# Weight conversion in pairs with an integer add, row sums from a ones column, fixed PSUM banks and another order of the beginning, in a kernel of local attention and two MLPs

## The chip, the cores and the metric

The kernel runs on one core of a Trainium2 chip. The metric is device time in microseconds (us) of one execution; the kernel before takes 1071.78 us (median of three runs). Engines are called as the profile calls them: PE (TensorE, matmul; PEld its weight loads), DVE (VectorE), ACT (ScalarE), POOL (GpSimd) and SP (SyncE, which here issues every DMA).

## What is computed

```python
# q, k, v: (4, 8, 768, 64) float32; mem_k, mem_v: 8 memory rows per head
for c in range(768 // 32):                        # chunks of 32 queries
    l, r = max(0, 32*c - 16), min(768, 32*c + 32 + 8)
    k_full = concat([mem_k, k[:, :, l:r]]); v_full = concat([mem_v, v[:, :, l:r]])
    s = q_c @ k_full.T / 8
    a = exp(s - s.max()); a = a / (a.sum() + 1e-9)
    out_c = a @ v_full
x = out.transpose(0, 2, 1, 3).reshape(3072, 512)
h = max(x @ w1, x @ w2, x @ w3)                    # 512 -> 768
y = h @ w_mid                                      # 768 -> 512
g = y @ w_in                                       # 512 -> 2048
g = where(g >= 1, g, where(g <= -1, 0, (g + 1)**2 / 4))
out = g @ w_out                                    # 2048 -> 512
```

The weights lie in DRAM as 64-bit floats. The kernel splits each matrix, activations too, into a high and a low part and multiplies with three matmuls (high by high, high by low, low by high).

## The kernel before, in words

**Work.** The 3072 tokens are 24 units of 128 and six blocks of 512 (four units each). Attention goes by unit `u`, in steps: `tk`/`ck` (transpose k on PE, copy out on ACT), `ek`, `kw` (windows of k), `tq`/`cq`, `s` (64 small score matmuls), `mx` (row maxima and subtraction, DVE), `ex` (exp, ACT), `n` (row sums, reciprocal, multiplication), `a`/`ca` (transpose), `o` (64 small matmuls with v), `co` (copy), `x`/`cx`/`dx` (transpose into the high and low halves of the MLP's input). `lk`, `lq`, `lv` load k, q and v. The first MLP takes 18 layer-one slots per block (`slot_l1`, three matrices by six 128-wide columns, 12 matmuls of 512 columns each) and six layer-two slots (`slot_l2`, also 12 matmuls); the second MLP takes 16 and 16 slots per block. All six blocks of the first MLP come before the second.

**Weights.** A 64-bit tile is fetched as 128x512 pairs of 32-bit words (`fetch_w`, 512 KB). The 24 tiles of the first MLP are made into high and low parts at the start, by `convert_w` (clear the sign, clamp, shift, merge: L137 to L143), `hi_w` (L150), `rest_w` (a correction from the lower word: L156 to L162), `sub_w` (L168) and `add_w` (L173), spread over DVE, ACT and POOL by lists of names. The 32 tiles of the second MLP are fetched and rounded to 32 bits by `round_w` (L180 to L182) between the slots of blocks 1 to 4, 30 of them are stored to DRAM (`wd`), loaded again later by `load_w` and split by `split_w`.

**Order.** Nothing is scheduled automatically: instructions run on each engine in the order of the program. `PLAN`, a list of names written out by hand, sets that order for the beginning: attention of units 0 to 3 whole and of units 4 to 8 in part, the 24 weight tiles, the first block's 18 layer-one slots (`l0` to `l17`) and five layer-two slots (`m0` to `m4`). `d` is a group of four matmuls whose result nobody reads (L723). From there on, the loop over `order` interleaves one slot, one attention step (`att_step`) and one piece of weight rounding (`round_step`).

**PSUM.** There are three pools: four banks that gather the layer-two sums, two for layer one, two for all else; in the beginning attention rotates over all of them (`psum_turn`).

Of the kernel before, what the change touches and what calls it, by code (L numbers as in the profile page):

```python
# [847 lines left out]
```

## Time and profile before

| what | value |
|---|---|
| runs | 1071.78, 1072.73, 1070.55 us; median 1071.78 |
| span of the profiled execution (first to last instruction) | 1066.3 us |
| PE busy | 1027.0 us, 96% of the span |
| DVE busy | 538.0 us, 50% |
| ACT busy | 347.8 us, 33% |
| POOL busy | 244.3 us, 23% |

The profile has no time of its own for the execution besides the span; the median of the runs lies 5.5 us above it. How to read it: PE is a pipeline and the ends of its matmuls are modelled, so the distance from one start to the next tells its pace, and a row's own duration does not. A row of the timeline gives the start, the duration, the engine and the line, and in brackets the idle time before it and what ended that.

### The profile page before, as it was taken

How to read it: one execution, taken by the hardware profiler on the slowest of the kernel's cores; microseconds unless marked ns; L12 is line 12 of the kernel's file. 1: busy time of each engine (PE TensorE's matmuls, PEld its weight loads, DVE VectorE, ACT ScalarE, POOL GpSimd, SP SyncE). 2: the span in 40 equal slices, each digit the busy share in tenths (PEclk: the TensorE clock that was granted, in tenths of full speed). 3: DMA queues.
4: the chain of work that ended last, by engine and by line, in shares of the span. 5: the costliest groups of instructions: out<-in, count | busy, mean ns of one | idle time of the engine just before them, and what ended most of it. 6: DMA issues, size and time to landing. Idle time of an engine off the chain costs nothing.

```text
span 1066.3 us, 18296 instructions
## 1 busy us (share of the span) xinstructions
PE 1027.0 (96%) x7426; PEld 833.3 (78%) x7426; DVE 538.0 (50%) x936; ACT 347.8 (33%) x625; POOL 244.3 (23%) x194
## 2 busy tenths in 40 slices
PE   5689999999999899999999999999999999999998
PEld 4467777888888787888888888888888888888886
DVE  7888975787776777734456232232222223223222
ACT  5744444333224223233343222222222222222222
POOL 2413231010110110102123323322322322332221
PEclk9669999999999999999999999999999999999999
DMA  9764415656646554333340010001001001001001
GB/s 225 185 175 126 128 32 154 153 142 150 153 117 151 144 137 144 108 108 114 124 138 21 11 50 12 19 19 41 20 1 50 23 8 50 21 1 40 1 1 39
DMA packets 163940, 88.89 MB, mean 83 GB/s; under 512 B 126736, under 2 KB 144144, under 8 KB 163856
## 3 DMA queue, kind: packets, MB, share of 16 engines
q1 hardware_dynamic: 163856, 87.72, 30.3%
q8 instruction: 58, 0.95, 0.4%
q14 instruction: 26, 0.21, 0.1%
HBM read 67.24 MB, written 20.45 MB: 82 GB/s over the span
## 4 chain that ended last, share of the span: by engine, by line
PE 88%; DVE 6%; issue 0%; POOL 0%; ACT 0%; POOLq 0%; DVEq 0%; ACTq 0%
PE l L512 17%; PE l L514 17%; PE l L513 17%; PE o L608 8%; PE o L610 8%; PE o L609 8%; PE y L512 3%; PE y L514 3%; PE y L513 3%; PE o L433 1%; PE s L368 1%; PE ta L420 1%; PE tx L447 1%; DVE lo_a L173 1%; DVE st_a L162 0%
## 5 line engine op out<-in xcount | busy, mean ns | idle before, releaser
L596 DVE SCALAR_TENSOR_TENSOR u<-u 128x512 f32<-128x512 f32 x96 | 66.6, 694 | 351.6 <-ACT u L595 351.6
L524 POOL TENSOR_TENSOR hl_b<-u,hh_b 128x512 fp32r<-128x512 f32 x96 | 124.0, 1291 | 373.3 <-ACT hh_b L522 215.8
L512 PE MATMUL l<-xh,hi_a 128*128 128x512 f32 x432 | 176.7, 409 | 2.8 <-DVE xh L455 1.6
L514 PE MATMUL l<-xh,lo_a 128*128 128x512 f32 x432 | 170.8, 395 | 2.6 <-DVE lo_a L173 2.6
L513 PE MATMUL l<-xl,hi_a 128*128 128x512 f32 x432 | 170.4, 394 | 0.0
L512 PE MATMUL l<-yh,hi_c 128*128 128x512 f32 x384 | 150.5, 392 | 0.0
L513 PE MATMUL l<-yl,hi_c 128*128 128x512 f32 x384 | 150.4, 392 | 0.0
L514 PE MATMUL l<-yh,lo_c 128*128 128x512 f32 x384 | 150.3, 391 | 0.0
L610 PE MATMUL o<-hi_d,hl_b 128*128 128x512 f32 x384 | 150.1, 391 | 0.0
L608 PE MATMUL o<-hi_d,hh_b 128*128 128x512 f32 x384 | 150.0, 391 | 0.0
L609 PE MATMUL o<-lo_d,hh_b 128*128 128x512 f32 x384 | 150.0, 391 | 0.0
L595 ACT ACTIVATE u<-l 128x512 f32<-128x512 f32 x96 | 57.4, 597 | 229.8 <-PE l L514 191.6
L524 POOL TENSOR_TENSOR hl_a<-t,hh_a 128x512 fp32r<-128x512 f32 x34 | 47.1, 1384 | 320.8 <-ACT hh_a L522 308.8
L522 ACT CAST hh_b<-u 128x512 fp32r<-128x512 f32 x96 | 59.6, 621 | 146.8 <-DVE u L597 146.8
L514 PEld LDWEIGHTS l<-xh,lo_a 128*128 128x128 f32 x432 | 82.1, 190 | 21.4 <-DVE lo_a L173 3.5
L512 PEld LDWEIGHTS l<-xh,hi_a 128*128 128x128 f32 x432 | 82.2, 190 | 21.2 <-DVE t L540 2.3
L513 PEld LDWEIGHTS l<-xl,hi_a 128*128 128x128 f32 x432 | 82.3, 190 | 15.7 <-DVE xl L459 0.4
L514 PEld LDWEIGHTS l<-yh,lo_c 128*128 128x128 f32 x384 | 72.3, 188 | 15.9
L513 PEld LDWEIGHTS l<-yl,hi_c 128*128 128x128 f32 x384 | 72.1, 188 | 15.8
L608 PEld LDWEIGHTS o<-hi_d,hh_b 128*128 128x128 f32 x384 | 72.1, 188 | 15.7 <-ACT y L565 0.2
L512 PEld LDWEIGHTS l<-yh,hi_c 128*128 128x128 f32 x384 | 72.1, 188 | 15.6
L609 PEld LDWEIGHTS o<-lo_d,hh_b 128*128 128x128 f32 x384 | 72.2, 188 | 15.4
(126 smaller groups left out, 1327.6 us busy)
## 6 DMA issues: line engine op xcount, KB each, us to landing
st_a<-in_moe_w_dram SPq DMA_DIRECT2D x18, 512.0 KB
vw<-in_v_dram SPq DMA_DIRECT2D x160, 56.0 KB
st_c<-in_moe_w_in_dram SPq DMA_DIRECT2D x16, 512.0 KB
st_d<-in_moe_w_out_dram SPq DMA_DIRECT2D x16, 512.0 KB
yd<-y SPq DMA_DIRECT2D x24, 256.0 KB
yr<-yd SPq DMA_DIRECT2D x24, 256.0 KB
out_dram<-ob SPq DMA_DIRECT2D x24, 256.0 KB
wd<-c_c SPq DMA_DIRECT2D x16, 256.0 KB
```

The source lines that it names most:

```text
L173: e.tensor_tensor(out=weights[kind, j][1], in0=c.bitcast(F32), in1=up.bitcast(F32), op=ALU.add)
L368: nc.tensor.matmul(s[e][c * CH:(c + 1) * CH, h * NK:(h + 1) * NK], qTb[u % 2][r, h, c], kw[r, h, c, 0:NK], start=True, stop=True)
L512: nc.tensor.matmul(ps, whi, xhi, start=first, stop=False)
L513: nc.tensor.matmul(ps, whi, xlo, start=False, stop=False)
L514: nc.tensor.matmul(ps, wlo, xhi, start=False, stop=last)
L522: nc.scalar.copy(out=hi, in_=h)
L524: e.tensor_tensor(out=lo, in0=h, in1=hi.bitcast(F32), op=ALU.subtract)
L595: nc.scalar.activation(out=a, in_=ps, func=AF.Relu, bias=0.5, scale=0.5)
L596: nc.vector.scalar_tensor_tensor(out=a, in0=a, scalar=1.0, in1=a, op0=ALU.min, op1=ALU.mult)
L608: nc.tensor.matmul(acc[t], hi[:, c], whi, start=first, stop=False)
L609: nc.tensor.matmul(acc[t], hi[:, c], wlo, start=False, stop=False)
L610: nc.tensor.matmul(acc[t], lo[:, c], whi, start=False, stop=last)
```

## The change

It has five parts. (1) Weights are handled in pairs of tiles (128x1024). The high word is cleared, clamped, shifted and merged as before, but the correction from the low word is now an integer: ACT multiplies the low word by 2^-29 and writes an integer (`tail_w`), and DVE adds it to the merged word (`sum_w`). High and low parts are then a copy on ACT (`wh`) and one subtraction (`ws`), on POOL but for the first two pairs. All 16 pairs of the second MLP now pass through DRAM. (2) The values get a 65th column of ones, so `o` also yields the row sums; the steps `n` are gone, and `co`, now on DVE, divides while it copies. (3) The eight PSUM banks are given by number. (4) `PLAN` is another: attention's inputs are loaded first and weights later, and there are more `d` groups. (5) y is reloaded in two pieces of 512 KB per block, not four of 256 KB.

```diff
-LEAST, MOST = 2.0 ** -15, float.fromhex("0x1.dffffep+16")
+LEAST, MOST = 2.0 ** -15, float.fromhex("0x1.dffffcp+16")
 PLAN = """
-f1 d7 lk1 wa1 lk0 f0 tk0 wg1 lq1 tk1 wa0 lmem0 wh1 ws1 wg0 mem0 lq0 lm0 lk2 ck0 tq0 tq1 ek0 ck1 wh0
...
+d3 lk0 d3 d3 d3 lmem0 d3 lq0 d3 d3 tk0 lk1 mem0 ck0 lm0 lq1 tq0 cq0 lk2 tk1 mv2 d3 ck1 d3 ek1 lk3
...
-        turn[0] += 1
-        if turn[0] % 4 == 3 and turn[0] < 54:
-            st = at.tile([P, TB, 2], U32, tag="st4", name=f"st_{kind}_{j}")
-        else:
-            st = stage.tile([P, TB, 2], U32, tag="st", name=f"st_{kind}_{j}", bufs=3)
+        if q not in staged:
+            staged[q] = stage.tile([P, 2, TB, 2], U32, tag="st", name=f"st{q}", bufs=2)
...
+    def abs_w(q, c):
+        nc.scalar.activation(out=c.bitcast(F32), in_=staged[q][:, :, :, 1].bitcast(F32), func=AF.Abs)
+
+    def tail_w(q):
+        low = staged[q][:, :, :, 0]
+        nc.scalar.activation(out=low, in_=low, func=AF.Copy, scale=2.0 ** -29)
+
+    def bits_w(q, c):
...
         V.tensor_scalar(out=cf, in0=cf, scalar1=LEAST, scalar2=MOST, op0=ALU.max, op1=ALU.min)
         V.tensor_scalar(out=c, in0=c, scalar1=3, scalar2=0x3FFFFFFF,
                         op0=ALU.logical_shift_left, op1=ALU.bitwise_and)
-        V.scalar_tensor_tensor(out=c, in0=up, scalar=0xC0000000, in1=c,
+        V.scalar_tensor_tensor(out=c, in0=staged[q][:, :, :, 1], scalar=0xC0000000, in1=c,
                                op0=ALU.bitwise_and, op1=ALU.bitwise_or)
-    def rest_w(kind, j):
...
-    def sub_w(kind, j):
...
-    def add_w(kind, j):
...
+    def sum_w(q, c):
+        nc.vector.tensor_tensor(out=c, in0=c, in1=staged.pop(q)[:, :, :, 0], op=ALU.add)
+
+    def new_c(q):
+        tiles[q] = stage.tile([P, 2, TB], U32, tag="c", name=f"c{q}", bufs=2)
+        return tiles[q]
...
+    def ws(q):
+        hi, lo = split2.pop(q)
+        e = nc.vector if f"ws{q}" in ON_DVE else nc.gpsimd
+        e.tensor_tensor(out=lo, in0=tiles.pop(q).bitcast(F32), in1=hi.bitcast(F32), op=ALU.subtract)
...
+    spots = {"s": (0, 1), "o": (2, 3), "a": 4, "x": 5, "k": 6, "q": 7}
...
-            nc.vector.tensor_reduce(out=r, in_=p, axis=AX.X, op=ALU.add)
-        nc.vector.tensor_scalar(out=r, in0=r, scalar1=1e-9, scalar2=None, op0=ALU.add)
-        nc.vector.reciprocal(out=r, in_=r)
-        e = nc.gpsimd if f"n{u}" in NORM_ON_POOL else nc.vector
-        e.tensor_tensor(out=p, in0=p, in1=r.to_broadcast([P, 2 * HP, NK]), op=ALU.mult)
...
-        for e, o in enumerate(pp.pop(("o", u))):
-            copy("co", u)(
-                out=xs[u].rearrange("p (h e d) -> p e h d", h=HP, e=2)[:, e],
-                in_=o[:, 0:HP * D].rearrange("p (h d) -> p h d", h=HP))
+        for e in range(2):
+            nc.vector.tensor_scalar(out=r[:, e], in0=o[e][:, :, D:D + 1], scalar1=1e-9, scalar2=None, op0=ALU.add)
+        nc.vector.reciprocal(out=r, in_=r)
+        for e in range(2):
+            nc.vector.tensor_tensor(
+                out=x[:, e], in0=o[e][:, :, 0:D], in1=r[:, e].to_broadcast([P, HP, D]), op=ALU.mult)
...
-    BY_PART = "out in b", "", "out in", "a", "b", "a"
+    BY_PART = "out in in", "", "", "a", "", "b"
...
             if name == "l0":
-                del psum_turn[:]
-                psum_turn += [(ps_t, "t")]
+                spots["k"], spots["q"] = spots["a"], spots["x"]
+            if name == "m0":
+                spots["s"] = spots["o"] = (4, 5)
```

**SP, the first DMAs.** `kq` takes k and q, `vw`, `vxh` and `vxl` take v, `st...` are weights, x8 are the eight DMAs of one unit's v. Before:

```order
L122 DMA st_a1_0_104<-in_moe_w2_dram 128x4x256
L223 DMA kq_87<-in_k_dram 128x8x64 x2
L122 DMA st_a0_0_118<-in_moe_w1_dram 128x4x256
L229 DMA kq_87<-in_q_dram 128x8x64
L691 DMA memk_93<-in_mem_k_dram 128x2x64 x2
L229 DMA kq_87<-in_q_dram 128x8x64
L237 DMA mv0_158<-in_mem_v_dram 8x4x64 x2
L223 DMA kq_87<-in_k_dram 128x8x64
L122 DMA st_a2_0_177<-in_moe_w3_dram 128x4x256
L223 DMA kq_87<-in_k_dram 128x8x64 x2
```

and in the changed kernel, from the first DMA to the second weight tile:

```order
L653 DMA memk_95<-in_mem_k_dram 128x2x64 x2
L217 DMA kq_89<-in_q_dram 128x8x64
L211 DMA kq_89<-in_k_dram 128x8x64
L225 DMA mv0_157<-in_mem_v_dram 8x4x64 x2
L217 DMA kq_89<-in_q_dram 128x8x64
L211 DMA kq_89<-in_k_dram 128x8x64 x2
L217 DMA kq_89<-in_q_dram 128x8x64 x2
L211 DMA kq_89<-in_k_dram 128x8x64
L243 DMA vw_92<-in_v_dram 40x4x64 x2
L243 DMA vw_92<-in_v_dram 56x4x64 x6
L120 DMA st0_332<-in_moe_w1_dram 128x4x256
L217 DMA kq_89<-in_q_dram 128x8x64
```

The first weight tile goes from the first place to behind the v of unit 0; five more v and k, q loads follow between the next tiles.

**DVE, two tiles of weights.** Before, the first two tiles (`a1_0` is the first of w2, `a0_0` the first of w1; `st` is the fetched tile, `c` the converted one):

```order
L140 TENSOR_SCALAR c_a1_0_112<-c_a1_0_112 128x512
L141 TENSOR_SCALAR c_a1_0_112<-c_a1_0_112 128x512
L143 SCALAR_TENSOR_TENSOR c_a1_0_112<-st_a1_0_104,c_a1_0_112 128x512
L156 TENSOR_SCALAR st_a1_0_104<-c_a1_0_112 128x512
L162 SCALAR_TENSOR_TENSOR st_a1_0_104<-st_a1_0_104 128x512
L140 TENSOR_SCALAR c_a0_0_133<-c_a0_0_133 128x512
L141 TENSOR_SCALAR c_a0_0_133<-c_a0_0_133 128x512
L143 SCALAR_TENSOR_TENSOR c_a0_0_133<-st_a0_0_118,c_a0_0_133 128x512
L168 TENSOR_TENSOR c_a1_0_112<-c_a1_0_112,hi_a1_0_140 128x512
L156 TENSOR_SCALAR st_a0_0_118<-c_a0_0_133 128x512
L162 SCALAR_TENSOR_TENSOR st_a0_0_118<-st_a0_0_118 128x512
```

In the changed kernel, the first pair (`c0`), unit 2's division (`r2`, `xs2`) and the second pair (`c1`):

```order
L141 TENSOR_SCALAR c0_606<-c0_606 128x1024
L142 TENSOR_SCALAR c0_606<-c0_606 128x1024
L144 SCALAR_TENSOR_TENSOR c0_606<-st0_332,c0_606 128x1024
L407 TENSOR_SCALAR r2_666<-bank2_81 128x4
L407 TENSOR_SCALAR r2_666<-bank3_82 128x4
L408 RECIPROCAL r2_666<-r2_666 128x8
L410 TENSOR_TENSOR xs2_667<-bank2_81,r2_666 128x4x64
L410 TENSOR_TENSOR xs2_667<-bank3_82,r2_666 128x4x64
L148 ISA c0_606<-st0_332,c0_606 128x2048
L141 TENSOR_SCALAR c1_684<-c1_684 128x1024
L142 TENSOR_SCALAR c1_684<-c1_684 128x1024
L144 SCALAR_TENSOR_TENSOR c1_684<-st1_507,c1_684 128x1024
```

The eleven instructions of two tiles (L168 of the second and both L173 stand further on) become four of 1024 columns per pair; the add at L148 is listed over 2048 elements. These first conversions stood ahead of the first scores and now stand behind those of unit 3.

**The copy between `o` and `x` in the loop after the plan.** Before, on ACT, for unit 10 (`o10_0`, `o10_1` are its two banks):

```order
L424 COPY aT10_2465<-ta10_2460 128x512
L137 ACTIVATE c_d_0_2472<-st_d_0_2393 128x512
L439 COPY xs10_2525<-o10_0_2491 128x4x64
L439 COPY xs10_2525<-o10_1_2492 128x4x64
L455 CAST xh2_2058<-tx10_2547 128x4x128
```

In the changed kernel, on DVE, the same unit's division behind a pair's conversion (`c14`) and the maxima of a slot (`t_1_3`):

```order
L519 TENSOR_TENSOR t_1_3_2228<-bank7_86,t_1_3_2228 128x512
L141 TENSOR_SCALAR c14_2264<-c14_2264 128x1024
L142 TENSOR_SCALAR c14_2264<-c14_2264 128x1024
L144 SCALAR_TENSOR_TENSOR c14_2264<-st14_1970,c14_2264 128x1024
L519 TENSOR_TENSOR t_1_3_2228<-bank6_85,t_1_3_2228 128x512
L407 TENSOR_SCALAR r10_2315<-bank4_83 128x4
L407 TENSOR_SCALAR r10_2315<-bank5_84 128x4
L408 RECIPROCAL r10_2315<-r10_2315 128x8
L410 TENSOR_TENSOR xs10_2316<-bank4_83,r10_2315 128x4x64
L410 TENSOR_TENSOR xs10_2316<-bank5_84,r10_2315 128x4x64
```

The copy moves from ACT, behind one weight instruction of 512 columns, to DVE, behind three of 1024 and a slot's maximum.

## Rows read from the trace of the kernel before

**Rows 1.** The page, part 1: busy time of each engine

```profile
PE 1027.0 (96%) x7426; PEld 833.3 (78%) x7426; DVE 538.0 (50%) x936; ACT 347.8 (33%) x625; POOL 244.3 (23%) x194
```

**Rows 2.** Stretches: length, busy (x count) per engine, granted clock, DMA share, GB/s

```profile
0.00:20.00 20.00, 8.68 (x95) 6.71 (x96) 13.27 (x36) 11.71 (x20) 3.81 (x10) 1.00 0.97 224
20.00:40.00 20.00, 11.95 (x321) 9.10 (x327) 19.35 (x40) 13.57 (x27) 7.50 (x6) 0.82 0.86 214
...
45.00:67.70 22.70, 17.16 (x339) 13.31 (x323) 17.35 (x39) 14.65 (x29) 7.30 (x6) 0.58 0.73 182
67.70:73.20 5.50, 5.46 (x12) 3.76 (x12) 5.33 (x10) 1.24 (x2) 0.00 (x0) 0.50 0.51 141
74.80:151.60 76.80, 71.83 (x688) 56.68 (x686) 68.64 (x119) 35.92 (x68) 22.16 (x16) 1.00 0.39 110
...
151.60:351.00 199.40, 198.67 (x2114) 159.68 (x2112) 138.13 (x265) 68.53 (x128) 24.18 (x19) 1.00 0.57 141
...
600.00:700.00 100.00, 100.00 (x440) 82.27 (x439) 27.38 (x40) 24.99 (x42) 28.18 (x22) 1.00 0.07 22
```

**Rows 3.** Timeline of PE: first layer-one matmul, a stall, end of the plan

```profile
67.75 0.76 PE L512 MATMUL l<-xh,hi_a 128*128 128x512 f32 x1 [1.63 <-DVE xh L455]
...
146.46 0.50 PE L514 MATMUL l<-xh,lo_a 128*128 128x512 f32 x1 [1.56 <-DVE lo_a L173]
...
151.59 0.39 PE L512 MATMUL l<-xh,hi_a 128*128 128x512 f32 x1
```

**Rows 4.** Chain that ended last: PE's pace in a score step and a transpose

```profile
165.89 0.44 PE tx L447 x4
...
169.08 0.79 PE s L368 x53
```

**Rows 5.** Timeline of DVE just ahead of the first layer-one matmul

```profile
65.24 0.43 DVE L156 TENSOR_SCALAR st_a<-c_a 128x512 uint32<-128x512 uint32 x1 [2.47 <-POOL c_a L168]
66.31 0.68 DVE L459 TENSOR_TENSOR xl<-tx,xh 128x512 fp32r<-128x512 f32 x1
```

**Rows 6.** Timeline of SP: eight issues of v each for units 0 and 3

```profile
23.31 6.24 SPq L255 DMA_DIRECT2D vw<-in_v_dram  x8
...
43.13 4.71 SPq L255 DMA_DIRECT2D vw<-in_v_dram  x8
```

**Rows 7.** Groups of DVE: count | busy us, mean ns of one | idle before

```profile
L388 DVE TENSOR_TENSOR p<-s,m 128x256 f32<-128x256 f32 x48 | 17.9, 413 | 0.0
...
L143 DVE SCALAR_TENSOR_TENSOR c_a<-st_a,c_a 128x512 uint32<-128x512 uint32 x18 | 12.5, 692 | 0.6
...
L141 DVE TENSOR_SCALAR c_c<-c_c 128x512 uint32<-128x512 uint32 x16 | 6.8, 428 | 0.5
```

**Rows 8.** Groups of ACT and POOL, same columns

```profile
L538 ACT COPY t<-l 128x512 f32<-128x512 f32 x36 | 21.1, 585 | 49.3 <-PE l L514 45.3 <-POOL hl_a L524 4.0
...
L439 ACT COPY xs<-o 128x256 f32<-128x256 f32 x48 | 15.5, 376 | 27.6 <-PE o L433 27.0 <-PE tx L447 0.6
...
L137 ACT ACTIVATE c_a<-st_a 128x512 f32<-128x512 f32 x13 | 8.9, 681 | 14.5 <-DMA st_a<-in_moe_w_dram 5.8 <-POOL lo_a L173 3.9 <-POOL lo_b L173 3.0
...
L173 POOL TENSOR_TENSOR lo_a<-c_a,st_a 128x512 fp32r<-128x512 f32 x6 | 8.2, 1363 | 9.0 <-DVE c_a L168 5.9 <-issue 2.7
```

**Rows 9.** Timeline of DVE and of POOL at 81 us

```profile
81.24 1.31 DVE L140 TENSOR_SCALAR c_a<-c_a 128x512 f32<-128x512 f32 x1
...
80.97 1.30 POOL L173 TENSOR_TENSOR lo_a<-c_a,st_a 128x512 fp32r<-128x512 f32 x1
```

**Rows 10.** Timeline at 350 us: DVE, then PE; and the stretch behind the stall

```profile
348.66 0.43 DVE L140 TENSOR_SCALAR c_c<-c_c 128x512 f32<-128x512 f32 x1 [5.54 <-DMA vw<-in_v_dram]
...
355.49 0.20 DVE L412 RECIPROCAL r<-r 128x8 f32<-128x8 f32 x1
...
356.57 0.63 PE L420 MATMUL ta<-ident,p 128*128 128x128 f32 x4 [2.61 <-DVE p L414]
...
356.50:360.30 3.80, 3.73 (x12) 3.04 (x13) 3.73 (x8) 1.17 (x2) 0.00 (x0) 0.59 0.83 189
```

More of the change, by code (lines that the diff above doesn't have):

```diff
@@ L100, in attention_then_two_mlps @@
     wd = dram.tile([2 * K2, P, TB], F32, name="wd")
+    banks = [psum.tile([P, TB], F32, name=f"bank{i}") for i in range(8)]
     weights = {}
@@ L142, in convert_w @@
                         op0=ALU.logical_shift_left, op1=ALU.bitwise_and)
-        V.scalar_tensor_tensor(out=c, in0=up, scalar=0xC0000000, in1=c,
+        V.scalar_tensor_tensor(out=c, in0=staged[q][:, :, :, 1], scalar=0xC0000000, in1=c,
                                op0=ALU.bitwise_and, op1=ALU.bitwise_or)
-        half[kind, j] = low, up, c
-    def hi_w(kind, j, pool):
-        hi = pool.tile([P, TB], F32R, tag="w", name=f"hi_{kind}_{j}")
-        lo = pool.tile([P, TB], F32R, tag="w", name=f"lo_{kind}_{j}")
-        nc.scalar.copy(out=hi, in_=half[kind, j][2].bitcast(F32))
-        weights[kind, j] = (hi, lo)
@@ L195, in split_w, with load_w @@
+    def load_w(q):
+        n = 2 * (q - Q1)
+        staged[q] = stage.tile([P, 2, TB], F32, tag="st", name=f"w{q}", bufs=2)
+        nc.sync.dma_start(out=staged[q], in_=wd[n:n + 2].rearrange("t p f -> p t f"))
+    def split_w(q, pool):
+        new_w(q, pool)
+        t = staged.pop(q)
+        hi, lo = split2.pop(q)
         nc.scalar.copy(out=hi, in_=t)
         nc.vector.tensor_tensor(out=lo, in0=t, in1=hi.bitcast(F32), op=ALU.subtract)
-        weights[kind, j] = hi, lo
     kT2 = at.tile([P, 2, HP, LEFT + P + RIGHT], F32, name="kT2")
@@ L508, in att_step, with mm3, next_mm @@
             run(*s)
-    def mm3(ps, whi, wlo, xhi, xlo, first, last):
-        nc.tensor.matmul(ps, whi, xhi, start=first, stop=False)
-        nc.tensor.matmul(ps, whi, xlo, start=False, stop=False)
-        nc.tensor.matmul(ps, wlo, xhi, start=False, stop=last)
-    hs, cur, acc = {}, {}, {}
+    def mm3(out, whi, wlo, xhi, xlo, first, last):
+        nc.tensor.matmul(out, whi, xhi, start=first, stop=False)
+        nc.tensor.matmul(out, whi, xlo, start=False, stop=False)
+        nc.tensor.matmul(out, wlo, xhi, start=False, stop=last)
+    hs, cur = {}, {}
+    acc = banks[0:KD]
+    mm_turn = [0]
+    def next_mm():
+        mm_turn[0] += 1
+        return banks[6 + mm_turn[0] % 2]
     unsplit, stores = [], []
@@ L662, in attention_then_two_mlps, with round_step @@
-    BY_PART = "out in b", "", "out in", "a", "b", "a"
-    def w_tile(n):
-        return conv[n][1] or bp["w"]
-    def w_step(s):
-        n = ready[0]
-        while asked[0] < min(stashed, n + 3) and asked[0] < converted[0] - len(stash):
+    def round_step(acts):
+        if "out" in acts and kept:
+            q, c = kept.pop(0)
+            n = 2 * (q - Q1)
+            nc.sync.dma_start(out=wd[n:n + 2].rearrange("t p f -> p t f"), in_=c)
+        q = rounded[0]
+        if "a" in acts and q in staged:
+            abs_w(q, new_c(q))
+            tail_w(q)
+            bits_w(q, tiles[q])
+        if "b" in acts and q in tiles:
+            sum_w(q, tiles[q])
+            kept.append((q, tiles.pop(q).bitcast(F32)))
+            rounded[0] += 1
+        if "in" in acts:
+            for _ in range(acts.count("in")):
+                if fetched[0] < len(conv) and fetched[0] // 2 - rounded[0] < 2:
+                    fetch_w(fetched[0])
+                    fetched[0] += 1
```

367 lines of the change are left out of this document (143 added, 224 removed).

## The prediction

> **What bounds the kernel now.** I read the page's shares first: PE is busy for 96% of the span [rows 1], so a change that leaves the matmuls as they are can only win where PE waits. The stretches show where that is [rows 2]. Late in the run PE is busy all the time, with 440 matmuls in 100 us: 0.227 us each, 2.73 us for a slot of 12. From 151.6 us PE is full already (198.67 of 199.40). Before that it is not: between 45 and 67.7 us it is busy for 17.16 of 22.70 at a granted clock of 0.58, and DVE has no gap from 20 to 40 us (19.35 of 20.00). The timeline of PE gives the marks [rows 3]: the first layer-one matmul starts at 67.75, released by DVE; the plan's last one is over at 151.59, where the loop's first slot begins. Between them PE waits again for a low part of the weights (1.56 us at 146.46). In 74.8 to 151.6 us DVE is busy for 68.64 of 76.80 and PE for 71.83: two engines about as full as one another [rows 2]. Just ahead of the first layer-one matmul DVE still handles weights and then xl [rows 5].
>
> So the beginning is 151.6 us, and the rest, 914.7 us of the span of 1066.3, is PE's. At 151.59 and at the same slot of the changed kernel the same slots and attention steps are done, so time = end of the plan + rest. The median lies 5.5 us above the span, in work outside it that the change does not touch; I predict differences and add them to the median.
>
> **The floor of the plan after its first slot.** PE then has 18 layer-one and five layer-two slots, 23 x 2.73 = 62.8 us; seven score and `o` steps at 0.79, 5.5; eleven transposes at 0.44, 4.8 [rows 2, 4]. That is 73 us. Before, it took 151.6 - 67.75 = 84.
>
> **Weights in pairs.** DVE takes 0.413 us for two inputs of 256 columns and 0.692 for 512 [rows 7]: 0.28 per 256 more, so 1.25 for 1024 and 2.37 for 2048. One input takes 0.428 for 512, about 0.73 for 1024 if its fixed part is the same. Before, two tiles cost DVE 2 x (0.43 + 0.43 + 0.69 + 0.43 + 0.69) = 5.3 us, and 0.69 for each subtraction that was not on POOL. Now a pair costs 0.73 + 0.73 + 1.25 = 2.7 and the integer add. The trace of before has no such add. If it runs as the merge does, a word at a time, it takes 1.25; if it steps through the 2048 elements it is listed with, 2.37. I take 1.5, nearer to the merge, which also reads every second word of the fetched tile, and keep both ends.
>
> The Trainium skill's page "VectorE: DVE Perf Modes" ("What auto-detection actually checks") says that the engine takes two elements a cycle if every tensor is 16-bit with step one. By that rule the add would cost about 1.2 us, an estimate; where the skipped words break the rule, 2.3. The row gives no answer, so this is rival C below.
>
> ACT's part is hidden: per pair a clearing (0.68 for 512, some 1.1 for 1024), the low word and a copy (0.585 for 512, 0.21 per 256 more, 1.0 each) [rows 8], 3.1 us against DVE's 4.2. POOL subtracts ten of twelve pairs at 2 x 1.363 = 2.7 us [rows 8], 27 us in the stretch, hidden too unless it holds DVE. It can: at 81.24 a clamp took 1.31 us instead of 0.43, while a POOL subtraction ran from 80.97 to 82.27 [rows 9]. So each of the ten may cost DVE between nothing and its length less what had passed; at most one clamp a pair, 0.9 as measured, 9 us over ten. I take half, 4.
>
> The Trainium skill's page "SBUF — State Buffer" ("SBUF: two separate sides") states that VectorE and GpSimd share a port pair under an exclusive lock, held for the whole instruction. The two rows at 81 us agree. By that rule a doubled subtraction can hold DVE for up to 2.7 us, 27 over ten; the sum would be some 20 us later at worst.
>
> **The order of the beginning.** Attention's data come first now. Ahead of the first layer-one slot there are some 15 loads of k and q (0.26 MB), four of v (0.43 MB) and five tiles (0.52 MB), 8.3 MB; at the 224 GB/s of the first 20 us [rows 2] that is 37 us. SP needs 4.7 to 6.2 us to issue one v [rows 6], 19 to 25 for four, and these start only behind the first loads, at some 14 us; I let the fourth v land at 41. Behind it come `o` 0.8, the division 1.4 (two multiplications of 0.413 and three small operations at 0.2 [rows 7, 10]), transpose 0.44, a cast of 0.4 on ACT, and xl 0.68 [rows 5]: 3.7 us. In DVE's queue there stand between them an add (1.5), a unit's maxima and subtractions (four operations like the 0.413 one, 1.65) and a subtraction of a pair (1.25): 4.4. So the first slot starts at about 50 us against 67.75. Bounds: 45 if those were all done before the v lands, 58 if SP's later queue is as slow as its slowest row and the half clock of before's first slot (granted 0.50 [rows 2]) shows again.
>
> From there DVE has ten pairs: 10 x (2.7 + 1.5) = 42 us; twelve layer-one maxima at 0.69, 8.3; four xl, 2.7; two subtractions of h, 1.4; four divisions, 5.7; three units' maxima, 5.0. That is 65, and with POOL's holds 69. The first of the ten begins some 4 us after the first slot, since a unit's maxima and the pair's landing stand ahead; after the last add there remain a copy on ACT (1.0), POOL's subtraction (2.7) and the two slots that stand behind it (5.5), 9 us. 4 + 69 + 9 = 82, above PE's floor of 73, so DVE sets it: the plan ends at 132, **19.6 us earlier**. With the add at 2.37 it is 141, with 1.25 and no holds 125.
>
> **The rest.** Matmuls stay; the ones column makes 64 small ones a column longer, nothing against 0.79 us. The stall at 356.57 goes if nothing is late there: 2.61 us, and 0.41 of the 3.8 us at a granted clock of 0.59 behind it, 1.6 [rows 10]; DVE had waited 5.54 us there for a DMA, ahead of `n`, which is gone. Fetches and conversions move, so I count 4. Against it stands the division. PE has one slot, 2.73 us, between `o` and the transpose that waits for it; the division takes 1.4, so 1.3 may be lost in DVE's queue. Behind it in order before were ACT's two copies of 0.376 [rows 8]; now a pair's three operations (2.7) and a maximum (0.69) may be running when `o` ends. The overshoot is nothing at best and 2.7 + 0.7 + 1.4 - 2.7 = 2.1 us at worst; I take 0.45 for the 16 units that have a conversion: 7 us. Net **+3**. The y reload moves the same bytes at a DMA share of 0.07 [rows 2]: nothing.
>
> Sum: 1071.8 - 19.6 + 3 = **1055 us**.
>
> **Rivals.** A, the forecast, DVE-bound plan: 0.60, with 1045 to 1063 of its own (first slot 45 to 58, holds 0 to 9, rest 0 to 7).
>
> B: the fetches become the bound. There are two pair buffers, so the fetch of a pair waits for the add of the pair two before. One turn is 1.05 MB at the plan's 110 to 141 GB/s (9.5 to 7.4 us [rows 2]), some 2 to land, then 1.1, 2.7 and 1.5: 14.7 to 16.8 us for two pairs, 73 to 84 for ten. The plan ends at 50 + 13 + 73 to 84, 136 to 147; the time is 1059 to 1070. For it: the DMA share of 0.73 to 0.97 early on. Against it: less v and k is left to load by then. 0.17.
>
> C: the add costs 1.25 and nothing is held; PE's floor sets the end, 50 + 73 = 123, and with nothing lost in the rest the time is 1071.8 - 28.6 = 1043. For it: the merge's row. 0.12.
>
> D, slower: the division sits between `o` and the transpose on the wrong queue. 19.6 + 4 us are won, so it decides from 24 / 16 = 1.5 us per unit. At the whole overshoot of 2.1, and a clamp held by POOL's subtraction of h in front of it (0.9 [rows 9]), it is 3.0 x 16 = 48, and the time 1071.8 - 24 + 48 = 1096; the clock may fall behind each stall as at 356. For it: DVE is busy for 138 of 199 us there [rows 2]. Against it: that is 69%, and much of it was rounding that is now cheaper. 0.11.
>
> **Range.** 1041 to 1069 takes in A, C and most of B, and leaves D and B's end out. Faster by over 0.2% (about what a measurement of this kernel can tell from none) is A, B and C but for what is left of them near 1070: 0.86; within it 0.03; slower 0.11.
>
> **What would show it.** Right: the first layer-one matmul near 50 us, the loop's first slot near 132, DVE over 90% busy between them; the integer add near 1.5 us; clamps of over 1.6 us beside POOL's subtractions; small PE gaps before the transposes of x after the plan. Wrong: DVE waiting for DMA of weights in the plan (B), the add at either end of its bounds, or gaps of over 1.5 us before the transposes of x (D).

## The result and the profile after

The changed kernel takes 1054.98 us (median of four runs, 1053.55 to 1055.62); the kernel before, measured beside it, 1071.16 (four runs, 1067.14 to 1072.73). The ratio is 0.986, its 95% interval 0.9836 to 0.9885: 12 to 18 us less. The span went from 1066.3 to 1053.3, 13.0 less. The forecast was 1055.

The page of the kernel after, part 1, answers [rows 1]:

```profile
PE 1027.2 (98%) x7542; PEld 832.3 (79%) x7542; DVE 456.7 (43%) x733; ACT 350.1 (33%) x545; POOL 227.7 (22%) x172
```

PE did the same work in 13 us less. The marks of its timeline, to set beside [rows 3] (first layer-one slot, a wait for a low part, first slot of the loop, and the one stall after it):

```profile
53.01 0.48 PE L484 MATMUL bank<-xh,hi 128*128 128x512 f32 x1
...
108.86 0.50 PE L486 MATMUL bank<-xh,lo 128*128 128x512 f32 x1 [0.86 <-POOL lo L173]
...
139.59 0.51 PE L484 MATMUL bank<-xh,hi 128*128 128x512 f32 x1 [0.68 <-ACT xh L425]
...
331.82 0.66 PE L417 MATMUL bank<-ident,xs 128*128 128x128 f32 x4 [1.56 <-DVE xs L410]
```

The first slot starts 14.7 us earlier, the plan ends 12.0 earlier, the rest is 1.0 shorter (913.7 against 914.7). So from the first slot to the end of the plan it now takes longer, 86.6 against 83.8. That is no loss: nine of the 24 weight tiles had passed DVE's merge before the first slot in the kernel before, four now, and the other twenty stand in those 86.6 us. What fell is DVE's work in all. From the start to the end of the plan, before (first row) and after (second fence), columns as in [rows 2]:

```profile
0.00:151.59 151.59, 119.38 (x1539) 93.08 (x1539) 128.08 (x249) 80.71 (x151) 43.36 (x40) 0.88 0.60 152
```

```profile
0.00:139.59 139.59, 120.06 (x1654) 93.97 (x1654) 105.92 (x175) 80.27 (x120) 31.91 (x22) 1.00 0.69 174
```

DVE does in 105.9 us what took 128.1, 22 less, and it set the time in both kernels: of the chain that ended last, 48 of the 83.8 us from the first slot to the end of the plan lie on DVE before, 56 of the 86.6 after, and after that is most of the stretch from 60.6 to 115 us. A piece of it (start, length, what):

```profile
66.75 0.60 DVE t L519
67.34 1.13 DVE c L148
68.48 0.60 DVE hl_a L503
69.08 0.01 issue
69.09 0.70 DVE c L141
69.79 0.02 issue
69.81 0.70 DVE c L142
70.52 0.02 issue
70.54 3.30 DVE c L144
```

The last line is a merge that takes 1.22 us elsewhere. The groups of DVE between the first slot and the end of the plan show how often that happened (count | busy, mean ns of one | idle before):

```profile
L144 DVE SCALAR_TENSOR_TENSOR c<-st,c 128x1024 uint32<-128x1024 uint32 x10 | 16.3, 1628 | 0.3
L141 DVE TENSOR_SCALAR c<-c 128x1024 f32<-128x1024 f32 x10 | 14.1, 1411 | 0.8 <-ACT c L133 0.7
L148 DVE CUSTOM_DVE_ANT_0 c<-st,c 128x2048 uint16<-128x2048 uint16 x10 | 13.8, 1380 | 1.0
L142 DVE TENSOR_SCALAR c<-c 128x1024 uint32<-128x1024 uint32 x10 | 9.0, 903 | 0.3
```

Their medians over the run are 1.226, 0.695, 1.221 and 0.694 us, 38.3 us for ten pairs; they took 53.2. The 14.9 us beyond lie beside POOL's instructions. DVE's timeline, and POOL's:

```profile
60.50 2.68 DVE L141 TENSOR_SCALAR c<-c 128x1024 f32<-128x1024 f32 x1
...
70.54 3.29 DVE L144 SCALAR_TENSOR_TENSOR c<-st,c 128x1024 uint32<-128x1024 uint32 x1
...
76.72 0.42 DVE L372 TENSOR_TENSOR p<-bank,m 128x256 f32<-128x256 f32 x1
77.07 0.41 DVE L371 TENSOR_REDUCE m<-bank 128x4 f32<-128x256 f32 x1
77.52 0.42 DVE L372 TENSOR_TENSOR p<-bank,m 128x256 f32<-128x256 f32 x1
77.86 1.48 DVE L519 TENSOR_TENSOR t<-bank,t 128x512 f32<-128x512 f32 x2
```

```profile
60.23 2.40 POOL L173 TENSOR_TENSOR lo<-c,hi 128x1024 fp32r<-128x1024 f32 x1 [58.78 <-ACT hi L168]
70.07 2.68 POOL L173 TENSOR_TENSOR lo<-c,hi 128x1024 fp32r<-128x1024 f32 x1 [7.44 <-ACT hi L168]
76.35 2.40 POOL L173 TENSOR_TENSOR lo<-c,hi 128x1024 fp32r<-128x1024 f32 x1 [3.60 <-ACT hi L168]
```

Eight of the ten subtractions held one conversion each, five of them clamps, for 12.9 us together; two merges lost 1.0 us each to POOL's subtractions of h. The clamp at 60.50 and the merge at 70.54 lose 2 us each to a subtraction that had begun just before. Beside the third one, from 76.35 to 78.75, DVE reads PSUM (`bank`) and loses nothing.

The granted clock is 1.00 in all of the first 140 us, where it was 0.88.

### The profile page after: what moved, and what is told of

Its sections match the earlier page's. It is cut to its first block, busy times and chain, and to the rows that moved or that the text cites. A ratio compares the mean times of both kernels' runs of the same rounds, so it can differ in the third digit from the quotient of the medians.

```text
span 1053.3 us, 17983 instructions
## 1 busy us (share of the span) xinstructions
PE 1027.2 (98%) x7542; PEld 832.3 (79%) x7542; DVE 456.7 (43%) x733; ACT 350.1 (33%) x545; POOL 227.7 (22%) x172
## 4 chain that ended last, share of the span: by engine, by line
PE 87%; DVE 7%; DMA 3%; SPq 1%; issue 1%; ACT 1%; POOL 0%; DVEq 0%; POOLq 0%; ACTq 0%
PE bank L484 19%; PE bank L485 19%; PE bank L486 19%; PE bank L597 8%; PE bank L596 8%; PE bank L595 8%; DVE c L144 1%; PE bank L397 1%; DVE c L148 1%; PE bank L355 1%; DVE c L141 1%; SPq L243 1%; DMA kq<-in_k_dram 1%; DVE c L142 1%; PE bank L417 1%
## 5 line engine op out<-in xcount | busy, mean ns | idle before, releaser
L484 PE MATMUL bank<-xh,hi 128*128 128x512 f32 x432 | 174.9, 405 | 1.2 <-ACT xh L425 0.7
L486 PE MATMUL bank<-xh,lo 128*128 128x512 f32 x432 | 168.9, 391 | 1.8 <-POOL lo L173 1.8
L485 PE MATMUL bank<-xl,hi 128*128 128x512 f32 x432 | 169.0, 391 | 0.3 <-DVE xl L429 0.2
L484 PE MATMUL bank<-yh,hi 128*128 128x512 f32 x384 | 150.4, 392 | 0.0
L485 PE MATMUL bank<-yl,hi 128*128 128x512 f32 x384 | 150.2, 391 | 0.0
L486 PE MATMUL bank<-yh,lo 128*128 128x512 f32 x384 | 150.2, 391 | 0.0
L597 PE MATMUL bank<-hi,hl_b 128*128 128x512 f32 x384 | 150.0, 391 | 0.0
L596 PE MATMUL bank<-lo,hh_b 128*128 128x512 f32 x384 | 149.9, 390 | 0.0
L595 PE MATMUL bank<-hi,hh_b 128*128 128x512 f32 x384 | 149.8, 390 | 0.0
L485 PEld LDWEIGHTS bank<-xl,hi 128*128 128x128 f32 x432 | 81.3, 188 | 15.9 <-DVE xl L429 1.0
L485 PEld LDWEIGHTS bank<-yl,hi 128*128 128x128 f32 x384 | 72.2, 188 | 15.8
```

The costliest lines, as they stand in the source:

```text
L484: nc.tensor.matmul(out, whi, xhi, start=first, stop=False)
L485: nc.tensor.matmul(out, whi, xlo, start=False, stop=False)
L486: nc.tensor.matmul(out, wlo, xhi, start=False, stop=last)
L595: nc.tensor.matmul(acc[t], hi[:, c], whi, start=first, stop=False)
L596: nc.tensor.matmul(acc[t], hi[:, c], wlo, start=False, stop=False)
L597: nc.tensor.matmul(acc[t], lo[:, c], whi, start=False, stop=last)
```

## The experiments

For all of them, from PE's timeline and the spans (us; rest = span less end of the plan):

| kernel | median | ratio to before, 95% | first slot | plan ends | between | rest |
|---|---|---|---|---|---|---|
| before | 1071.16 | | 67.75 | 151.59 | 83.8 | 914.7 |
| after | 1054.98 | 0.9836 to 0.9885 | 53.01 | 139.59 | 86.6 | 913.7 |
| no fillers | 1055.44 | 0.9852 to 0.9885 | 53.95 | 140.53 | 86.6 | 913.0 |
| subtractions on DVE | 1051.12 | 0.9813 to 0.9845 | 52.02 | 134.45 | 82.4 | 913.5 |
| half subtractions | 1053.04 | 0.9833 to 0.9877 | 50.81 | 137.50 | 86.7 | 912.7 |
| add twice | 1068.74 | 0.9983 to 1.0003 | 52.71 | 152.53 | 99.8 | 913.2 |
| old correction | 1090.72 | 1.0190 to 1.0238 | 55.65 | 169.96 | 114.3 | 918.6 |
| row sums back | 1063.41 | 0.9928 to 0.9964 | 56.01 | 152.38 | 96.4 | 910.9 |
| longer division | 1075.68 | 1.0048 to 1.0086 | 50.89 | 138.92 | 88.0 | 933.5 |
| before, with fillers | 1072.73 | 1.0028 to 1.0063 | 69.85 | 157.76 | 87.9 | 914.1 |
| weights first again | 1061.32 | 0.9896 to 0.9943 | 55.39 | 143.61 | 88.2 | 916.2 |
| old correction on DVE | 1083.28 | 1.0125 to 1.0155 | 53.78 | 161.90 | 108.1 | 919.6 |
| three edits | 1045.59 | 0.9768 to 0.9815 | 50.29 | 131.29 | 81.0 | 911.3 |
| two beside PSUM | 1046.10 | 0.9765 to 0.9804 | 54.68 | 134.62 | 79.9 | 911.4 |

Beside the later ones the kernel before took 1068.0 to 1069.6. The column of the first slot has a spread of its own: the program is the same up to there in the kernel after, with the subtractions on DVE, with the longer division and in the last two, and it starts at 50.3 to 54.7, as the loads land. The column "between" leaves that out, and the plan's edits are judged by it, but it has a spread too: the longer division touches nothing in the plan, and its 88.0 stands beside the 86.6 of the kernel after. The difference is the granted clock behind a wait of 1.7 us that both have:

```profile
129.25 0.84 PE L397 MATMUL bank<-vw,aT 64*32 64x65 f32 x62 [1.73 <-DVE xl L429]
```

```profile
127.14 1.05 PE L397 MATMUL bank<-vw,aT 64*32 64x65 f32 x62 [1.70 <-DVE xl L429]
```

In the 4 us from there on it is 1.00 in the kernel after (first fence) and 0.57 with the longer division (second), which makes the 1.4 us between them. So differences of up to 1.5 us in that column say nothing of an edit.

**The fillers.** All `d` steps are taken out of `PLAN`:

```diff
-d3 lk0 d3 d3 d3 lmem0 d3 lq0 d3 d3 tk0 lk1 mem0
+lk0 lmem0 lq0 tk0 lk1 mem0
...
```

> The changed kernel without its filler groups (the matmuls whose result nobody reads). Theory 1, the fillers keep TensorE's granted clock at full in the first 70 us and cost nothing: without them the granted clock falls to about 0.6 to 0.8 somewhere between 20 and 60 us as in the kernel before, the first layer-one slot runs at half clock (5.5 us for 12 matmuls), the first slot comes 1 to 4 us later than at 53.0 and the whole is 4 to 8 us slower (1059 to 1063). Theory 2, DVE and the loads set the time of the first slot and the clock is beside the point: within 1.5 us of 1055. Theory 3, the fillers hold PE up: first slot 1 to 3 us earlier, 1052 to 1054.

Stretches of this kernel (columns as in [rows 2]; the clock stands before the DMA share):

```profile
20.00:40.00 20.00, 11.73 (x345) 8.60 (x344) 9.04 (x23) 8.28 (x14) 0.00 (x0) 0.68 0.76 189
40.00:53.95 13.95, 10.79 (x228) 8.65 (x227) 12.08 (x26) 12.24 (x19) 0.00 (x0) 0.60 1.02 251
53.95:60.00 6.05, 5.99 (x29) 4.69 (x28) 5.74 (x9) 4.68 (x9) 0.00 (x0) 1.00 0.55 119
```

The clock falls as theory 1 says, yet the first slot is 0.9 us later and at full clock, and the time is the same: theory 2. PE is busy for 11.7 of the 20 us there even so; it waits for loads and for DVE. The 0.9 us lie inside the spread of that mark.

The opposite edit on the kernel before puts 33 more groups (the text below counts 34) ahead of steps at which PE waited:

```diff
-f1 d7 lk1 wa1 lk0 f0 tk0
+f1 d7 lk1 wa1 lk0 f0 d8 d8 d8 d8 tk0
...
```

> The kernel before, its only edit 34 more filler groups ahead of 15 early steps of PE at which it waited. Theory 1, DVE sets the time of the first layer-one slot there: the granted clock rises to 0.9 to 1 between 20 and 68 us, the first slot starts 0 to 4 us earlier than at 67.75 and is no longer at half clock (2.7 us), so the time is 3 to 7 us less than the kernel before. Theory 2, the clock was most of the gain: 9 to 13 us less. Theory 3, the fillers take PSUM banks and PE time that the steps want: no gain or slower.

The clock from 20 to 40 us rose from 0.82 to 1.00 and the first slot ran at full clock, but 2 us later, and the time is 0.3 to 0.6% more. Theory 3, for the result. The first slot takes 2.7 us less, but PE then waits for DVE's maximum, where the kernel before has no wait of over 1.6 us behind its first slot:

```profile
84.42 0.50 PE L497 MATMUL l<-xh,hi_a 128*128 128x512 f32 x1 [3.46 <-DVE t L525]
```

From 85.5 to 89.5 us, behind that wait, the granted clock is 0.57. Neither run shows the clock ahead of the first slot as a part of the gain.

**What DVE's time is worth.** In the first MLP the integer add is done twice:

```diff
-        nc.vector.tensor_tensor(out=c, in0=c, in1=staged.pop(q)[:, :, :, 0], op=ALU.add)
+        low = staged.pop(q)[:, :, :, 0]
+        for _ in range(2 if q < Q1 else 1):
+            nc.vector.tensor_tensor(out=c, in0=c, in1=low, op=ALU.add)
```

> The integer add of the twelve pairs of the first MLP is done twice, so the correction enters twice there; nothing else is changed. It measures what 1.22 us more of DVE per pair costs. Theory 1, DVE sets the plan from 60 us to the last add: ten adds lie there, 12 us more, less what falls into POOL's holds and into DVE's waits (up to 4): the plan ends 8 to 12 us later, time 1063 to 1067. Theory 2, PE or the fetches set the plan: 0 to 4 us later, 1055 to 1059.

The stretch grew by 13.2 us for ten adds of 1.22: a microsecond of DVE there is one of the kernel. DVE was busy 11.8 us longer; the granted clock of the stretch, 0.95 for 1.00, may be the rest. Theory 1, a little above its range (1068.7, plan over 12.9 later).

**The integer add.** The old correction, with the subtraction and addition on POOL, and then on DVE:

```diff
-        nc.scalar.activation(out=low, in_=low, func=AF.Copy, scale=2.0 ** -29)
...
-        nc.vector.tensor_tensor(out=c, in0=c, in1=staged.pop(q)[:, :, :, 0], op=ALU.add)
+        V.tensor_scalar(out=up, in0=c, scalar1=0xFF800000, scalar2=None, op0=ALU.bitwise_and)
+        V.scalar_tensor_tensor(out=up.bitcast(F32), in0=low, scalar=2.0 ** -52, in1=up.bitcast(F32),
+                               op0=ALU.mult, op1=ALU.mult)
...
+        e.tensor_tensor(out=c, in0=c, in1=hi.bitcast(F32), op=ALU.subtract)
+        e.tensor_tensor(out=lo, in0=c, in1=up, op=ALU.add)
```

> The changed kernel with the correction of before: for each pair DVE extracts the exponent (one input, 1024 columns, 0.7 us) and multiplies the lower word (two inputs, 1.23) in place of the integer add (1.22); in the first MLP the subtraction is followed by an addition on the same engine, in the second the addition is on DVE (1.23); ACT no longer scales the lower word. Pairs, order, ones column and fillers stay. Theory 1, DVE's chain sets the plan, POOL's instructions hold it, and a pair's buffer is free only after POOL's addition: 7 us more on DVE, 5 to 15 more of holds, so the plan ends 10 to 22 us later and the time is 1065 to 1077: the integer add is most of the gain. Theory 2, the order and the fillers made the gain: 0 to 6 us later, 1055 to 1061.

> The old correction in pairs once more, but with the subtraction and the addition of every pair on DVE instead of POOL. The same beside the run with all subtractions on DVE (1051, plan over at 134.5) shows the price of the correction alone: 0.7 + 1.23 + 1.22 against the integer add's 1.22, 1.9 us more per pair. Theory 1, DVE's chain sets the plan, the buffers do not: ten pairs, 17 to 21 us more, plan over at 151 to 156, with up to 8 us beside it for the second MLP's pairs, time 1068 to 1078. Theory 2, the pair buffers, held longer, set it: plan over at 160 to 170 as with POOL, 1080 to 1090. Theory 3, the correction did not matter and POOL's two steps were the whole loss: plan over at 135 to 142, 1052 to 1060.

The first lost more than theory 1 said: the plan ends 30 us later, the time is 2% above the kernel before. The second lands in theory 2's range (161.9, 1083.3), but mostly by what theory 1 counts: measured from the first slot it is 25.7 us longer than with the integer add and the subtractions on DVE (108.1 against 82.4). DVE's own work explains 20.9 of them (94.5 us busy against 73.6, theory 1's 19). The other 4.8 are waits: DVE waits for ACT's first instruction of a pair (7.2 us in all, 0.2 with the integer add), and ACT for the fetch. ACT's first instruction of a pair in this kernel, and the same in the kernel after (waits of ACT from the first slot on: us, times, longest):

```profile
ACT c L133 <- DMA st<-in_moe_w_dram: 22.8, 5, 8.9
ACT hh_a L509 <- DVE t L527: 9.1, 4, 6.1
ACT c L133 <- DMA st<-in_moe_w_out_dram: 8.1, 2, 5.7
```

```profile
ACT c L133 <- DMA st<-in_moe_w_dram: 1.7, 2, 0.9
```

SP issues a fetch when the pair's buffer is free: here it waits for that until the last addition (L181; four waits, 17.2 us), in the kernel after until the integer add (L148; four waits, 14.7 us). This is rival B, in a kernel where a pair's buffer is held until the last addition. With the integer add the fetched pair is done with when the add ends. So the add does two things: it takes DVE's time down, and with it two buffers of a pair suffice. No run has a third buffer, so the price of the buffers alone is not shown.

**The ones column.** `n` is put back behind `ex`, and `co` is two copies on ACT:

```diff
+    def st_n(u):
+        p = pt[u].rearrange("p h e j -> p (h e) j")
+        nc.vector.tensor_reduce(out=r, in_=p, axis=AX.X, op=ALU.add)
...
-                out=x[:, e], in0=o[e][:, :, 0:D], in1=r[:, e].to_broadcast([P, HP, D]), op=ALU.mult)
+            nc.scalar.copy(out=x[:, e], in_=o[e][:, :, 0:D])
```

> The changed kernel with the step of before between exp and transpose (row sum, reciprocal and multiplication of p on DVE, 2.1 us a unit), and the division after the values replaced by two copies on ACT; the ones column stays but is not read. Theory 1, the ones column matters where DVE sets the pace: about 0.7 us more of DVE per unit in the plan (2.1 against 1.4), and the transpose of p waits for DVE as before; 3 to 8 us slower, 1058 to 1063. Theory 2, the change of the step only moves it along the chain: within 2 us of 1055.

1063.4, theory 1, just over its upper end. The plan ends 12.8 us later: 3.0 at the first slot, 9.8 behind it, of which one stall of `o` on DVE is

```profile
97.16 1.18 PE L392 MATMUL bank<-vw,aT 64*32 64x65 f32 x62 [5.39 <-DVE xl L419]
```

Part of the 9.8 is not waiting but a lower clock: in three stretches of 3.5 to 4 us behind waits of PE (from 56.0, 97.2 and 142.0 us) the granted clock was 0.50 to 0.53, where the kernel after has 1.00. That is up to 5.5 us, an estimate from these lengths and clocks. The rest is 2.8 us shorter than in the kernel after (910.9); the stall at 331.8, 1.56 us in front of the transpose behind the division, is not there.

**The division in the loop.** Its two multiplications are done three times in units 9 to 23:

```diff
-        for e in range(2):
+        for e in (0, 1, 0, 1, 0, 1) if u > 8 else (0, 1):
             nc.vector.tensor_tensor(
...
```

> In the loop after the plan (units 9 to 23) the two multiplications of the division are done three times, 1.7 us more on DVE between the values and the transpose of x; the values do not change. It measures the slack there. Theory 1, the working of the prediction: PE has a slot of 2.73 us in between, the division takes 1.4, so 1.3 us are to spare and each of the 15 units stalls by 0.4 us or more when nothing stands ahead and by over 2 where a pair's conversion does: 8 to 25 us slower, 1063 to 1080. Theory 2, PE's order leaves more room than one slot: 0 to 4 us slower, 1055 to 1059.

Every unit now stalls, most of them like this:

```profile
196.07 0.66 PE L417 MATMUL bank<-ident,xs 128*128 128x128 f32 x4 [1.01 <-DVE xs L410]
216.81 0.66 PE L417 MATMUL bank<-ident,xs 128*128 128x128 f32 x4 [1.23 <-DVE xs L410]
```

15 stalls, 18.1 us, against one of 1.56 in the kernel after; the rest grew by 19.8. 1.7 us more of DVE cost 1.0 to 1.2, so 0.5 to 0.7 us were to spare, not the 1.3 of theory 1, but no conversion stood in the way either: only one stall exceeds the others (2.75), the one that the kernel after has too; behind it the granted clock was 0.57 for 4 us.

**The order of the beginning.** The first two pairs go back to where weights stood before:

```diff
-d3 lk0 d3 d3 d3 lmem0 d3 lq0 d3 d3 tk0 lk1 mem0 ck0 lm0 lq1 tq0
+f0 d3 lk0 d3 d3 d3 lmem0 d3 lq0 d3 d3 tk0 lk1 f1 mem0 ck0 lm0 lq1 f2 tq0
...
-s0 tk2 lq2 mx0
+wa0 wr0 wc0 wd0 s0 tk2 lq2 mx0 wh0 ws0
...
-mx1 a0
+mx1 wa1 wr1 wc1 wd1 a0
```

> The changed kernel with only the place of the first two pairs put back to where weights stood before: their four tiles are fetched between the first loads of k and q, the first pair is converted ahead of the first scores on DVE, the second ahead of unit 1's transpose; all else stays. Theory 1, the new place is what brings the first layer-one slot forward: 2.1 MB ahead of q and v delay attention by up to 9 us (2.1 MB at 224 GB/s) and DVE's first maxima wait behind a conversion that waits for its tile: the first slot comes 4 to 9 us later than at 53.0, the time is 3 to 9 us more (1058 to 1064). Theory 2, the same bytes must land before the first slot in any order, and DVE is half idle in the first 40 us: first slot within 2 us of 53, time within 2 us of 1055, or up to 5 less since DVE has two conversions behind it.

1061.3, in theory 1's range, but the first slot is only 2.4 us later, half of its lower bound, and inside the spread of that mark. What is clear is the whole (ratio 0.9896 to 0.9943, above the kernel after's interval) and a wait that it puts on PE early on:

```profile
20.42 1.12 PE L238 MATMUL bank<-ident,kq 128*128 128x128 f32 x4 [5.02 <-ACT kT L241]
```

ACT's copy of k stands there behind the copy of the first pair's high part, which had waited 3.89 us for DVE's add. Of the 6 us, 2.4 lie ahead of the first slot, 1.6 behind it in the plan and 2.5 in the rest (916.2). The 1.6 are a granted clock of 0.64 for 4.5 us behind a wait of 1.73 us for xl like the two shown above, which the kernel after passes at full clock. The 2.5 are the one stall behind the plan, here 2.33 us long instead of 1.56, and a clock of 0.63 for 4.6 us behind it. So only the 2.4 us, and the wait above, can be put down to the place of the two pairs; whether the lower clock would come again with it is not shown.

**POOL's subtractions.** All on DVE, and, apart from that, issued in halves on POOL:

```diff
-mem0 mv0 mv1 mv2 mv6 lha0_0 lha0_2 ws0 ws1
+mem0 mv0 mv1 mv2 mv6 lha0_0 lha0_2 ws0 ws1 ws2 ws3 ws4 ws5 ws6 ws7 ws8 ws9 ws10 ws11
```

> The subtractions of the pairs 2 to 11 go from POOL to DVE. Theory 1, DVE's chain sets the plan and POOL's subtractions hold it: ten subtractions of 1.22 us are added to DVE (12.2), the holds beside the subtractions (13 of the 14.9 us by which the conversions ran over their undisturbed times) go, and the low part comes 1.2 us earlier after the last add: the plan ends 0 to 3 us earlier, time 1052 to 1055. Theory 2, the holds fall into time in which DVE would have waited anyway: the added 12 us lengthen the plan by 5 to 12, time 1060 to 1067.

```diff
+        for i in range(2):
+            e.tensor_tensor(out=lo[:, i], in0=c[:, i], in1=hi[:, i].bitcast(F32), op=ALU.subtract)
```

> Each subtraction of a pair is issued as two of 512 columns instead of one of 1024, on the same engine. Theory 1, a POOL instruction holds DVE's for as long as it lasts and DVE gets in between two: a held conversion loses at most 1.3 us instead of up to 2.1, the holds of the plan fall from 14.9 us to 6 to 10, the plan ends 3 to 7 us earlier, time 1048 to 1052. Theory 2, POOL's second half holds the next DVE instruction for as long again: holds 13 to 17 us, time 1054 to 1057.

With them on DVE the same groups take (and one more, the subtraction):

```profile
L144 DVE SCALAR_TENSOR_TENSOR c<-st,c 128x1024 uint32<-128x1024 uint32 x10 | 14.2, 1421 | 0.3
L148 DVE CUSTOM_DVE_ANT_0 c<-st,c 128x2048 uint16<-128x2048 uint16 x10 | 12.2, 1221 | 0.7
L173 DVE TENSOR_TENSOR lo<-c,hi 128x1024 fp32r<-128x1024 f32 x10 | 12.2, 1220 | 0.0
...
L142 DVE TENSOR_SCALAR c<-c 128x1024 uint32<-128x1024 uint32 x10 | 6.9, 694 | 0.3
L141 DVE TENSOR_SCALAR c<-c 128x1024 f32<-128x1024 f32 x10 | 6.8, 685 | 0.0
```

The conversions fell from 53.2 to 40.1 us, the subtractions brought 12.2: DVE is about where it was, and "between" is 4.2 us shorter, of which DVE's busy time makes 2.1 (73.6 against 75.7) and its waits the rest: PE no longer waits for low parts from POOL (twice, 1.8 us, in the kernel after). Theory 1, and a little better. Halving did not help: "between" is the same 86.7, the holds fell only from 14.9 to 12.7 us, and POOL's work rose from 25.0 to 30.2 (20 of 1.53). The 2 us of the median are within the two intervals and go with an earlier first slot. Theory 2.

**A faster kernel.** The subtractions on DVE, `mv6` (copies of memory values) on ACT, and one DMA more per step of the loop from the queue of k and q:

```diff
-mem0 mv0 mv1 mv2 mv6 lha0_0 lha0_2 ws0 ws1
+mem0 mv0 mv1 mv2 lha0_0 lha0_2 ws0 ws1 ws2 ws3 ws4 ws5 ws6 ws7 ws8 ws9 ws10 ws11
...
-                feed((4, 5, 3, 5, 4, 0)[part])
+                feed((5, 6, 4, 6, 5, 0)[part])
```

> Three edits of the changed kernel at once: the subtractions on DVE (as in the run that gave 1051), the copies of memory values of unit 6 on ACT instead of DVE (1.4 us of DVE at 114), and one DMA more per step of the loop from the queue of k and q loads (to bring in k before DVE waits for it at 326). DVE sets the plan: over at 133 to 134.5; if the late k was behind the stall at 331.8 it goes (1.6 us), otherwise it stays or moves: time 1048 to 1051. If more DMAs per step hold back the fetches or the v loads, new stalls of PE after 140 us and 1051 to 1056.

1045.6, ratio 0.9791: clear of the kernel after, and below what was expected (1048 to 1051, plan over at 133 or later). The plan ends 8.3 us earlier (2.7 of that at the first slot) and the stall at 331.8 is gone, as is DVE's wait of 4.73 us for k ahead of it; the rest is 2.4 us shorter. In the kernel after that wait ends at 326.07, less than 6 us ahead of the stalled transpose, and a pair's clamp, shift and merge (2.6 us) run on DVE in between. The kernel with only the subtractions on DVE still has the stall (1.75 us), so that edit does not remove it; the other two were not run apart.

Last, the finding on PSUM: of these three edits' subtractions those of pairs 4 and 8, behind which DVE only reads PSUM, go back to POOL.

> The three edits of the run that gave 1045.6, but the subtractions of pairs 4 and 8 go back to POOL. Behind the adds of these two pairs DVE has only instructions that read PSUM (division, maxima) while POOL works. Theory 1, POOL holds only DVE instructions whose operands all lie in SBUF (from 76.35 to 78.75 us, beside a POOL subtraction, the maxima of a unit and of a slot took their usual 0.41, 0.42 and 0.7): no instruction beside pair 4's subtraction is longer than usual, beside pair 8's at most one by 0.8, DVE saves 1.6 to 2.4 and the plan ends 1 to 2.5 us earlier than the 131.3, at 129 to 130.5; time 1043 to 1045. Theory 2, it holds whatever DVE does: 2.4 us each, the plan ends 2 to 4 later, 1047 to 1050.

POOL's two subtractions, and DVE beside the second:

```profile
76.53 2.41 POOL L173 TENSOR_TENSOR lo<-c,hi 128x1024 fp32r<-128x1024 f32 x1 [75.07 <-ACT hi L168]
...
104.56 2.43 POOL L173 TENSOR_TENSOR lo<-c,hi 128x1024 fp32r<-128x1024 f32 x1 [22.58 <-ACT hi L168]
```

```profile
104.70 0.41 DVE L371 TENSOR_REDUCE m<-bank 128x4 f32<-128x256 f32 x1
105.15 0.42 DVE L372 TENSOR_TENSOR p<-bank,m 128x256 f32<-128x256 f32 x1
105.49 0.68 DVE L519 TENSOR_TENSOR t<-bank,t 128x512 f32<-128x512 f32 x1
106.09 1.45 DVE L141 TENSOR_SCALAR c<-c 128x1024 f32<-128x1024 f32 x1
```

For the holds it is as theory 1 says: nothing beside the first, one clamp of 1.45 (0.77 over) beside the second. DVE was busy 2.0 us less (70.3 against 72.2), "between" fell by 1.1 us, which is inside its spread; the profiled execution's first slot came 4.4 later, so its plan ended at 134.6, and the runs, 1046.1 against 1045.6, tell no difference. The mechanism is shown, its worth is too small to be told here.

## Why the prediction was right, and where it was not

The number was right, and that it came within 0.3 us of the sum (1055.2) is luck: the plan won 7.6 us less than forecast, while the rest came out 4.0 better and the base 3.8.

- **What bounds it**: right. DVE sets the plan; the doubled add (13.2 us for 12.2) and the chain show it. DVE was busy for 87% between the two marks, though, not over 90%.
- **First slot at 50**: 53.0, inside 45 to 58. Up to there the chain lies on DMA and SP's issues for 26 of the 53 us and on DVE for 14. Which part of the change brought it forward is not shown: with one part undone it starts at 53.8 to 56.0, never near 67.75.
- **The integer add at 1.5**: 1.22. It runs like the merge, at the lower bound, 2.8 us less in ten pairs. The Trainium skill's rule ("VectorE: DVE Perf Modes", "What auto-detection actually checks") gave 1.2 as an estimate, and the trace agrees, although only every second word of the fetched tile is read; it does not prove the rule, since one 32-bit word at a time, as in the merge (1.226), takes as long.
- **POOL's holds at 4**: the term that was mis-sized. They took 14.9 us. "At most one clamp a pair, 0.9 as measured", halved, was taken as it stood from a POOL instruction of half the length. The clamp at 60.50, caught as early (0.27 us into the subtraction, as at 81.24 before), lost 2.0; a hold takes up to 2.1 us, also of shifts, merges and adds, eight of ten pairs have one, and POOL's h takes part. The Trainium skill's page "SBUF — State Buffer" ("SBUF: two separate sides") says that the lock lasts for the whole instruction; the merge of 3.29 us beside a subtraction of 2.68 agrees. The 14.9 lie between the 9 of the one row and that rule's worst case of 27.
- **82 from the first slot to the end of the plan**: 86.6, so the plan ends at 139.6, not 132, and 12.0 us are won there, not 19.6. DVE is busy for 75.7 of them (forecast 69: the holds 10.9 more, the add 2.8 less), and 10.9 are waits (forecast 13).
- **The rest at +3**: -1.0. The 7 us for the division were counted from conversions in its way; in the kernel after one of the 16 units in the loop stalls. The stall near 350 did not go, it moved to 331.8 and shrank from 2.61 to 1.56; no lower clock followed.
- **The base**: the median stood 5.5 us above the profiled span, and this was read as work outside the span that stays. It was not: wherever a run has its own span on record, its time is 1.7 to 2.2 us above it, in the kernel before 1.7 to 1.8. So the profiled execution was a quick one, some 1068 us (an estimate from its span), beside a median of 1071.8. Of the sum's 16.6, the spans show 13.0; the interval of the runs, 12 to 18, holds both, and beside the later measurements of the kernel before (1068.0 to 1069.6) it is 13 to 15.
- **Rivals**: C had the right price for the add, but not "nothing held". B did not come, ACT waited 1.7 us for fetched weights, but waits of this kind came with the old correction, which holds the buffers longer. D did not come either, by 0.5 to 0.7 us a unit.

The parts of the change are not a sum. Undone alone, the integer add costs 28 to 36 us, the ones column 8, the place of the first two pairs 6 (some 3 without the lower clock), the fillers nothing: more than the 16 that all bring. Pairs with the old correction are slower than the tiles of before (ratios 1.02 and 1.01), so the pairs did not pay without the add; the add without the pairs was not run, nor were the numbered PSUM banks, the way of all pairs through DRAM and the reload of y undone.

## What to carry to other kernels

Where one engine is the chain, count its time with what holds it: price an instruction on POOL by the DVE instructions with operands in SBUF that will stand beside it, not by POOL's idle time. Moving ten subtractions of 2.5 us from the free POOL to the full DVE made the stretch 4.2 us shorter. Before a few microseconds are put down to an edit, look at the granted clock: behind the same wait it fell in one execution and not in another. And a cheaper operation that ends a buffer's life early can be worth more than its time; look for who waits for that buffer.
